# Moving a third block of an output weight from one wide load into small transfers issued by GpSimd

## The chip, the cores and the metric

One core of a Trainium2 chip. The metric is the device time of one execution in microseconds; the kernel before takes 680.46 us (median of 3 runs, 680.43 to 680.58).

## The reference

One decoding step, batch 8, width 512, all float32. The normalised input goes into a grouped-query attention over a cache of 4096 keys (32 heads, 8 key-value heads, 128 wide) and into a gated MLP; the result is `x + s * g`.

```python
xn = layernorm(x)                                   # [8, 1, 512]
# attention
q = (xn @ wq) -> 32 heads of 128
scores = q . k_cache * 128**-0.5                    # k_cache, v_cache: [8, 8, 4096, 128]
s = softmax(scores) . v_cache -> [8, 1, 4096] @ wo  # wq [512, 4096], wo [4096, 512]
# gated MLP
z = gelu(xn @ w_in)                                 # w_in [512, 1792]
z1, z2 = z[:896], layernorm(z[896:])
g = silu((z1 * (w_sp * z2 + b_sp)) @ w_out)         # w_out [896, 512]
out = x + s * g
```

## The kernel before, in words

All data passes once from HBM to SBUF: wq, w_mlp, the caches k and v, and wo. The bulk goes through a ring of three slots of 64 KB a partition (`slot()`, `bufs=3`). SP issues the loads in the order of the program: wq, x, `w_mlp` (w_in, part of w_out and some side data), four loads `w_ex0` to `w_ex3`, then for each of the 8 key-value heads two halves of k and two of v (8 MB each, 64 KB a partition), and at the end wo in pieces, the first one ahead of the last v. A load waits on SP until PE has finished with the slot that it takes. The first v load takes the slot of w_mlp, so it waits until the MLP is done with it.

For each head PE forms the scores (line 269), DVE and ACT the softmax, PE the values (line 310). The two projections of q (line 249) and the whole MLP (`mlp()`) run ahead of the first head. The last pieces of wo are multiplied as they arrive (`project_o`, `direct`), and the result is stored.

w_out has 896 rows, seven blocks of 128 (`NB`). The hidden vector u is held as four groups of 32 partitions (`G`, `R`) by 256 columns (`FQ`), so group g holds blocks 2g and 2g + 1. Two blocks (`MOVED`, blocks 1 and 3) are not in w_mlp. They are brought by the four w_ex loads into a few partitions of the tile `w_ex`, seven units (`UNITS`) of 512 columns side by side; the rest of `w_ex` is zeroed by GpSimd first (line 98). `LANES` gives for each load its place, its number of fours of partitions, and its units. The sources hold a fifth, unused row after each four, so that their leading dimension is the number of fours.

In the MLP the kept blocks are used through `hT`, two transposes of u (line 206, copied out at 207) with one product a block (line 224). For the moved blocks the columns of u are copied to matching columns of a zeroed tile `spread` (lines 210 and 213), which is transposed unit by unit (line 217), copied (`hE`, line 219) and multiplied with `w_ex` (line 228). All add up in `pw`.

GpSimd issues no DMA. It has memsets, a part of the identity and two powers (lines 149 and 199).

Of the kernel before, what the change touches and what calls it, by code (L numbers as in the profile page):

```python
# [1 line left out]

# [6 lines left out]
F32 = mybir.dt.float32  # L9
# [4 lines left out]
P = 128  # L14
B, D = 8, 512
HKV, REP, S, DH = 8, 4, 4096, 128
NK = D // P
G = 4
J = S // (G * P)
R = 32  # L20
FH = 896
FQ = 256
NB = FH // P
MOVED = 2
QUAD = 4
UNITS = 7
LANES = [(0, 5, 0, 6), (1, 5, 0, 5), (1, 3, 5, 2), (0, 3, 6, 1)]
EPS = 1e-5
GELU_C = 0.7978845608028654
HALF = B // 2  # L30
# [7 lines left out]
AHEAD = FOLDED + 2  # L38


def lane_runs():
    f = 0
    for e, k, u, n in LANES:
        m = k * QUAD
        at, end = f, f + n * m
        while at < end:
            g = at // P
            stop = min(end, (g + 1) * P)
            unit, lo = divmod(at - f, m)
            if lo or stop - at < m:  # L50
                whole, size = 1, min(m - lo, stop - at)
            else:
                whole, size = (stop - at) // m, m
            yield g, at - g * P, u + unit, whole, e * R + lo, size
            at += whole * size
        f = end


@with_exitstack
def tile_gqa_gmlp_decode(ctx: ExitStack, tc: tile.TileContext, x, kT, v, wq, wo, w_mlp, w_ex0, w_ex1, w_ex2, w_ex3, out, gate, stored):  # L60
    nc = tc.nc
    head = ctx.enter_context(tc.tile_pool(name="head", bufs=1))
    l = head.tile([P, HKV], F32, name="l")
# [4 lines left out]
    const = ctx.enter_context(tc.tile_pool(name="const", bufs=1))  # L68
# [5 lines left out]
    def slot():  # L74
        return ring.tile([P, SLOT], F32, name="slot")
# [5 lines left out]
    mlp_slot = slot()  # L81
    n_in, n_out = NK * 2 * FH, (NB - MOVED) * D
    n_mlp = n_in + n_out + P
    w_in_sb = mlp_slot[:, :n_in].rearrange("p (k n) -> p k n", k=NK)
    w_out_sb = mlp_slot[:, n_in:n_in + n_out].rearrange("p (j d) -> p j d", j=NB - MOVED)
    side_sb = mlp_slot[:, n_in + n_out:n_mlp]
    spare = [n_mlp]

    def from_slot(rows, n):
        lo = spare[0]  # L90
        spare[0] = lo + n
        return mlp_slot[:rows, lo:lo + n]
# [1 line left out]
    x_sb = from_slot(B, D)  # L94
    nc.sync.dma_start(x_sb, x)
    nc.sync.dma_start(mlp_slot[:, :n_mlp], w_mlp)
    w_ex = from_slot(2 * R, UNITS * D).rearrange("p (u d) -> p u d", u=UNITS)
    nc.gpsimd.memset(w_ex, 0.0)
    for (e, k, u, n), src in zip(LANES, (w_ex0, w_ex1, w_ex2, w_ex3)):
        nc.sync.dma_start(w_ex[e * R:e * R + k * QUAD, u:u + n], src[:, :QUAD])  # L100


    ident = const.tile([P, P], F32, name="ident")
    make_identity(nc, ident)
# [29 lines left out]
    def scratch(shape, name):  # L134
        t = ps.tile([P, 512], F32, name="scr")
        n = 1
        for s in shape[1:]:
            n *= s
        return t[:shape[0], :n]
# [18 lines left out]
    def mlp():  # L158
        zu = work.tile([P, 2, 2, FQ], F32, name="zu", tag="p")
        z, u_sb = zu[:, 0], zu[:, 1]  # L160
        rest = work.tile([P, 2 * D], F32, name="rest", tag="pT")
        hT, y_sb = rest[:, :2 * P], rest[:, D:]
        hT = hT.rearrange("p (a s) -> p a s", a=2)
        pz = scratch([P, 2 * FQ], "pz")
        nc.vector.memset(pz, 0.0)
        pz_v = pz.rearrange("p (a f) -> p a f", a=2)
        w_in_v = w_in_sb.rearrange("p k (a f) -> p k a f", a=2)
        for k in range(NK):
            for g in range(G):
                lo = g * FQ  # L170
                n = min(FQ, FH - lo)
                nc.tensor.matmul(pz_v[R * g:R * (g + 1), :, :n], xnT[:, k, :],
                                 w_in_v[:, k, :, lo:lo + n], start=(k == 0), stop=(k == NK - 1))
        zf, uf = z.rearrange("p a f -> p (a f)"), u_sb.rearrange("p a f -> p (a f)")
        nc.vector.tensor_copy(zf, pz)
        nc.vector.tensor_mul(uf, zf, zf)
        nc.vector.tensor_scalar(uf, uf, 0.044715, 1.0, op0=ALU.mult, op1=ALU.add)
        nc.vector.tensor_mul(uf, uf, zf)
        nc.scalar.activation(uf, uf, AF.Tanh, scale=GELU_C)
        nc.vector.tensor_scalar(uf, uf, 1.0, 0.5, op0=ALU.add, op1=ALU.mult)  # L180
        nc.vector.tensor_mul(zf, uf, zf)

        def mean(src, name, eps=0.0):
            part_sum = small.tile([P, 1], F32, name="part_sum")
            nc.vector.tensor_reduce(part_sum, src, op=ALU.add, axis=AX.X)  # L185
            pm = scratch([P, 1], "pm")
            nc.tensor.matmul(pm, same_all, part_sum, start=True, stop=True)  # L187
            t = small.tile([P, 1], F32, name=name)
            nc.vector.tensor_scalar(t, pm, 1.0 / FH, eps, op0=ALU.mult, op1=ALU.add)
            return t  # L190

        z1, z2 = z[:, 0, :], z[:, 1, :]
        mu = mean(z2, "mu")
        nc.vector.tensor_scalar(z2, z2, mu, None, op0=ALU.subtract)
        nc.vector.tensor_mul(u_sb[:, 0, :], z2, z2)
        nc.vector.memset(u_sb[(G - 1) * R:, 0, FH - (G - 1) * FQ:], 0.0)
        var = mean(u_sb[:, 0, :], "var", EPS)
        rs = small.tile([P, 1], F32, name="rs")
        nc.gpsimd.tensor_tensor(rs, var, neg_half, op=ALU.pow)
        nc.vector.tensor_scalar(z2, z2, rs, None, op0=ALU.mult)  # L200
        nc.vector.tensor_scalar(z2, z2, side_sb[:, W:W + 1], side_sb[:, W + 1:W + 2],
                                op0=ALU.mult, op1=ALU.add)
        nc.vector.tensor_mul(u_sb[:, 1, :], z2, z1)
        for a in range(2):
            th = scratch([P, P], "th")
            nc.tensor.transpose(th, u_sb[:, 1, a * P:(a + 1) * P], ident)  # L206
            nc.vector.tensor_copy(hT[:, a, :], th)
        wide = MOVED * R
        spread = from_slot(wide, UNITS * 2 * R).rearrange("p (u s) -> p u s", u=UNITS)
        nc.gpsimd.memset(spread, 0.0)  # L210
        for g, f, u, n, lo, m in lane_runs():
            rows = slice(R * g, R * (g + 1))
            nc.vector.tensor_copy(spread[rows, u:u + n, lo:lo + m],
                                  u_sb[rows, 1, P + f:P + f + n * m].rearrange("p (u s) -> p u s", u=n))
        te = scratch([2 * R, UNITS * wide], "te")
        for i in range(UNITS):
            nc.tensor.transpose(te[:, i * wide:(i + 1) * wide], spread[:, i, :], ident[:wide, :wide])  # L217
        hE = from_slot(2 * R, UNITS * wide)
        nc.vector.tensor_copy(hE, te)
        pw = scratch([P, D], "pw")  # L220
        kept = [j for j in range(NB) if j % 2 == 0 or j // 2 >= MOVED]
        for i, j in enumerate(kept):
            g, a = divmod(j, 2)
            nc.tensor.matmul(pw[R * g:R * (g + 1), :], hT[:, a, R * g:R * (g + 1)], w_out_sb[:, i, :],  # L224
                             start=(a == 0), stop=False)
        for i in range(UNITS):
            lo = wide * (i % 2)
            nc.tensor.matmul(pw[lo:lo + wide, :], hE[:, i * wide:(i + 1) * wide], w_ex[:, i, :],  # L228
                             start=False, stop=(i >= UNITS - 2))
        nc.vector.tensor_copy(y_sb, pw)  # L230
        py = scratch([P, W], "py")
        for g in range(G):
            for a in range(2):
                nc.tensor.matmul(py[R * g:R * (g + 1), :], pick[:, a, :],
                                 y_sb[:, (2 * g + a) * W:(2 * g + a + 1) * W], start=(a == 0), stop=(a == 1))
        nc.vector.tensor_copy(x_out, side_sb[:, :W])
        e = work.tile([P, W], F32, name="e", tag="o_all")
        nc.vector.tensor_scalar(e, py, -1.0, 87.0, op0=ALU.mult, op1=ALU.min)
        nc.scalar.activation(e, e, AF.Exp)
        nc.vector.tensor_scalar(e, e, 1.0, None, op0=ALU.add)  # L240
        nc.vector.reciprocal(e, e)
        nc.vector.tensor_mul(gate, py, e)
# [57 lines left out]
    turn = [0]  # L300
# [46 lines left out]
    project_q(0)  # L347
    project_q(1)
    mlp()
    for h in range(HKV):  # L350
        for half in range(2):
# [3 lines left out]
        for half in range(2):  # L355
# [11 lines left out]
            n = 2 if last else HALF  # L367
# [28 lines left out]
    for a in range(2):  # L396
        for g in range(G):
            c = (2 * g + a) * W
            nc.tensor.matmul(acc[R * g:R * g + OUT_ROWS, :], pick[:, a, :OUT_ROWS], part_f[:, c:c + W],
                             start=False, stop=False)  # L400
# [54 lines left out]
```

## Time and profile before

| | |
|---|---|
| median of 3 runs | 680.46 us (680.43 to 680.58) |
| profiled execution | 680.28 us |
| its span, first to last instruction | 678.8 us |
| granted TensorE clock, mean | 0.75 |
| busy PE / weight loads / DVE / ACT / GpSimd | 344.0 / 92.5 / 83.4 / 13.4 / 7.9 us |
| bytes read from HBM | 290.80 MB, 428 GB/s over the span |
| DMA packets | 6741, of which 6576 on the queue q1 |

The profile's DMA part has a row for each queue with packets, megabytes and the time of the packets as a share of sixteen engines' span. q1 holds the loads that SP issues, q8 and q14 the fetches of instructions, q10 the store at the end. A packet's record has a queue, a start, a duration and a size, and no engine number. In a view by stretches, the last two numbers of a row are the busy share of the sixteen DMA engines and the GB/s; packets are counted by their start, so that a share over a short stretch may pass 1.

### The profile page before, as it was taken

To read this page: it belongs to the slowest core of one execution; us is meant where nothing else is said; L and a number is where in the kernel's file an instruction comes from. 1 tells how busy PE (TensorE), PEld (TensorE's weight loads), DVE (VectorE), ACT (ScalarE), POOL (GpSimd) and SP (SyncE) were. 2 spreads that over 40 slices of the span, in tenths; PEclk is the share of its full clock that TensorE was granted. 3 is DMA by queue.
4 is the path that set the end of the run, shared out by engine and by line. 5 is a ranking of instruction groups with operands and counts; after the bars stand their busy time and mean duration, and the time that the engine had idled before them with its cause. 6 is when DMAs were issued, how large, how long until landed. Compare 5 with 4: busy or idle time off the path is not lost.

```text
span 678.8 us, 5218 instructions
## 1 busy us (share of the span) xinstructions
PE 344.0 (51%) x2415; PEld 92.5 (14%) x2415; DVE 83.4 (12%) x159; ACT 13.4 (2%) x27; POOL 7.9 (1%) x17
## 2 busy tenths in 40 slices
PE   0448744446655454555554344555544345555567
PEld 0112211111111011111111011111111011111111
DVE  1143021102110021101100021101101021100221
ACT  0010000000000000000000000000000000000000
POOL 3000000000000000000000000000000000000000
PEclk9987866787776568777666778877666787876679
DMA  9999999999999999999999999999999999999997
GB/s 386 453 441 430 430 433 430 433 430 433 434 433 430 433 433 430 433 441 440 434 433 430 436 436 434 440 434 433 430 433 430 433 433 434 430 436 433 419 427 315
DMA packets 6741, 291.16 MB, mean 429 GB/s; under 512 B 888, under 2 KB 888, under 8 KB 1688
## 3 DMA queue, kind: packets, MB, share of 16 engines
q1 hardware_dynamic: 6576, 290.80, 99.1%
q8 instruction: 19, 0.31, 0.2%
q10 hardware_dynamic: 144, 0.03, 0.0%
q14 instruction: 2, 0.02, 0.0%
HBM read 290.80 MB, written 0.03 MB: 428 GB/s over the span
## 4 chain that ended last, share of the span: by engine, by line
DMA 79%; PE 16%; issue 4%; DVE 0%; SPq 0%; POOLq 0%; POOL 0%
DMA slot<-in_kT 36%; DMA slot<-in_v 33%; PE sc L269 7%; PE o_ps L310 7%; DMA slot<-in_wo 7%; DMA slot<-in_x 3%; PE scr L224 1%; PE scr L228 1%; SPq L332 0%; PE scr L217 0%; DVE st L146 0%; POOLq L449 0%; POOL rstd L149 0%; PE scr L206 0%; PE acc L391 0%
## 5 line engine op out<-in xcount | busy, mean ns | idle before, releaser
L269 PE MATMUL sc<-slot,qz 128*32 128x512 f32 x1024 | 145.4, 731 | 131.2 <-DMA slot<-in_kT 131.2
L310 PE MATMUL o_ps<-slot,pT 128*16 128x512 f32 x1024 | 148.2, 743 | 110.0 <-DMA slot<-in_v 110.0
L269 PEld LDWEIGHTS sc<-slot,qz 128*32 128x32 f32 x1024 | 38.1, 131 | 232.0 <-issue 149.4
L310 PEld LDWEIGHTS o_ps<-slot,pT 128*16 128x16 f32 x1024 | 32.9, 114 | 211.0 <-issue 151.5
L274 DVE TENSOR_REDUCE nm<-sc 128x1 f32<-128x1024 f32 x8 | 9.8, 1225 | 273.7 <-PE sc L269 273.7
L313 DVE TENSOR_TENSOR o_all<-o_ps,diag 128x512 f32<-128x512 f32 x17 | 11.8, 692 | 244.8 <-PE o_ps L310 244.8
L276 ACT ACTIVATE p<-sc,nm 128x1024 f32<-128x1024 f32 x8 | 8.9, 1114 | 551.8 <-DVE nm L274 551.8
L320 PE MATMUL po_ps<-fold,o_sb 128*128 128x16 f32 x30 | 6.0, 274 | 26.8 <-DVE o_sb L315 26.8
L315 DVE TENSOR_REDUCE o_sb<-o_all 128x128 f32<-128x512 f32 x17 | 17.8, 1047 | 0.6
L153 PE MATMUL scr<-ident,slot 8*128 8x8 f32 x4 | 0.6, 254 | 25.0 <-DVE slot L150 25.0
L320 PEld LDWEIGHTS po_ps<-fold,o_sb 128*128 128x128 f32 x30 | 4.5, 189 | 40.6 <-DVE o_sb L315 40.6
L296 DVE STREAM_TRANSPOSE pT<-p 128x1024 f32<-128x1024 f32 x8 | 10.0, 1246 | 0.3
L249 PE MATMUL scr<-slot,xnT 128*32 128x512 f32 x64 | 8.9, 708 | 0.3 <-issue 0.3
L344 PE MATMUL sc<-slot,oT 128*8 128x512 f32 (+1 forms) x60 | 8.4, 565 | 1.1 <-DMA slot<-in_wo 1.0
L279 PE MATMUL scr<-ident,nm 128*1 128x128 f32 x8 | 2.2, 270 | 10.8 <-DVE nm L274 10.8
L292 PE MATMUL scr<-wl,same 128*128 128x1 f32 x16 | 3.6, 297 | 6.5 <-DVE wl L290 6.5
L294 DVE TENSOR_SCALAR p<-p,w,wl 128x1024 f32<-128x1024 f32 x8 | 6.5, 813 | 0.3
L224 PE MATMUL scr<-slot,rest 128*32 128x512 f32 x10 | 5.4, 1044 | 0.0
L187 PE MATMUL scr<-part_sum,same 128*128 128x1 f32 x4 | 1.1, 348 | 8.4 <-DVE part_sum L185 8.4
L285 PE MATMUL scr<-ident,full 1*128 1x1 f32 x8 | 1.8, 220 | 5.0 <-DVE full L283 5.0
L292 PEld LDWEIGHTS scr<-wl,same 128*128 128x128 f32 x16 | 3.2, 249 | 7.0 <-PE scr L285 7.0
L153 PEld LDWEIGHTS scr<-ident,slot 8*128 8x128 f32 x4 | 0.5, 208 | 25.0 <-DVE slot L150 25.0
(94 smaller groups left out, 69.0 us busy)
## 6 DMA issues: line engine op xcount, KB each, us to landing
slot<-in_v SPq DMA_DIRECT2D x2, 4096.0 KB, 28.7
slot<-in_w_mlp SPq DMA_DIRECT2D x1, 4928.0 KB, 32.7
slot<-in_wo SPq DMA_DIRECT2D x1, 2048.0 KB
slot<-in_wo SPq DMA_DIRECT2D x1, 1536.0 KB
slot<-in_wo SPq DMA_DIRECT2D x1, 1280.0 KB, 37.9
slot<-in_wo SPq DMA_DIRECT2D x1, 1024.0 KB
slot<-in_wo SPq DMA_DIRECT2D x4, 256.0 KB, 18.7
slot<-in_wo SPq DMA_DIRECT2D x1, 768.0 KB
```

Source lines behind the costliest of these rows:

```text
L224: nc.tensor.matmul(pw[R * g:R * (g + 1), :], hT[:, a, R * g:R * (g + 1)], w_out_sb[:, i, :], start=(a == 0), stop=False)
L249: nc.tensor.matmul(pq[R * g:R * (g + 1), :], xnT[:, k, :], wq_sb[:, k, lo:lo + REP * DH], start=(k == 0), stop=(k == NK - 1))
L269: nc.tensor.matmul(sc[R * g:R * (g + 1), c, :], qz[:, h, b * R:(b + 1) * R], k_sb[:, i, c, g, :], start=(b == 0), stop=(b == B - 1))
L274: nc.vector.tensor_reduce(m, sc, op=ALU.max, axis=AX.XY, negate=True)
L276: nc.scalar.activation(p, sc.rearrange("p c s -> p (c s)"), AF.Exp, bias=m, accum_out=l[:, h:h + 1])
L292: nc.tensor.matmul(tot, same_all, wl, start=True, stop=True)
L296: nc.vector.transpose(pT.rearrange("p j b g r -> p j g b r"), p.rearrange("p (j g b r) -> p j g b r", j=J, g=G, b=B))
L310: nc.tensor.matmul(of[R * c:R * c + G * REP, :], pT[:, j, b0 + i], v_sb[:, i, j], start=(j < rows), stop=(j >= J - rows))
L313: nc.vector.tensor_mul(o_all, o, diag[:, :, None].to_broadcast([P, G, DH]))
L315: nc.vector.tensor_reduce(o_sb, o_all.rearrange("p g d -> p d g"), op=ALU.add, axis=AX.X)
L320: nc.tensor.matmul(po[:, b0 * REP:(b0 + n) * REP], o_sb, f.rearrange("p i r -> p (i r)"), start=True, stop=True)
L344: nc.tensor.matmul(part[R * q:R * q + B, i * n:(i + 1) * n], oT[:, h, r, :], wo_sb[:, m, i * n:(i + 1) * n], start=(m < REP), stop=(cuts = ...
```

## The change

`MOVED` goes from 2 to 3: block 5 leaves w_mlp as well. Its rows are brought by GpSimd-issued transfers: `w_mid` into partitions 60 to 67, and `w_one0` to `w_one3` into three partitions each. Between these stand four transfers `skip` of a few bytes from w_mlp into a tile `turn` that nothing reads. The nine are kept in their written order (`tc.issue_after`). By the words of the change, the five are transfers of one and two shares into the partitions of DMA engines 7, 8 and 15: w_mid is two shares, of engines 7 and 8, and the w_ones are one share each, of engine 15, 7, 8 and 15 in this order.

`w_ex` now spans 128 partitions, its zeroing too. The four loads on SP bring the same bytes to the same partitions as before, but which row of w_out lies where has changed: a list `RUNS`, written out, gives for each run of columns its group, first column, first unit, units, first partition and count. `spread` has 32 rows instead of 64 and 128 columns a unit instead of 64; it is filled by 11 copies instead of 6. The unit's product has 32 stationary columns instead of 64 and adds to one group of `pw`; which group follows from the unit's number. One transpose of u remains of two, and four kept products of five.

In the order of instructions, the first skip is GpSimd's first work after the constants; the zeroing of `w_ex` and a memset of the identity follow, then the other eight transfers (the ninth waits for the first one's completion), and then the rest of the identity, the memsets and the first power. On DVE, the sums built from the identity (same, fold, diag) now stand behind the statistics of x and ahead of the instruction that normalises x. SP's order is unchanged.

```diff
-MOVED = 2
+MOVED = 3
 QUAD = 4
 UNITS = 7
-LANES = [(0, 5, 0, 6), (1, 5, 0, 5), (1, 3, 5, 2), (0, 3, 6, 1)]
+LANES = [(0, 20, 0, 6), (32, 20, 0, 5), (32, 12, 5, 2), (0, 12, 6, 1)]
+ONES = [(93, 0, 7), (29, 0, 5), (96, 0, 5), (124, 0, 7)]
+RUNS = [(0, 0, 0, 6, 0, 20), (0, 120, 0, 1, 60, 8), (1, 0, 0, 5, 29, 23), (1, 115, 6, 1, 0, 12),
+        (1, 127, 0, 1, 124, 1), (2, 0, 1, 6, 60, 8), (2, 48, 5, 2, 32, 12), (2, 72, 0, 5, 93, 6),
+        (2, 102, 5, 2, 93, 3), (2, 108, 0, 1, 125, 2), (2, 110, 1, 6, 124, 3)]
...
-    w_ex = from_slot(2 * R, UNITS * D).rearrange("p (u d) -> p u d", u=UNITS)
+    w_ex = from_slot(P, UNITS * D).rearrange("p (u d) -> p u d", u=UNITS)
     nc.gpsimd.memset(w_ex, 0.0)
-    for (e, k, u, n), src in zip(LANES, (w_ex0, w_ex1, w_ex2, w_ex3)):
-        nc.sync.dma_start(w_ex[e * R:e * R + k * QUAD, u:u + n], src[:, :QUAD])
+    for (p, m, u, n), src in zip(LANES, (w_ex0, w_ex1, w_ex2, w_ex3)):
+        nc.sync.dma_start(w_ex[p:p + m, u:u + n], src[:, :QUAD])
+    turn = const.tile([4 * QUAD, 4, QUAD], F32, name="turn")
+    queued = []
+
+    def queue(dst, src):
+        with tc.issue_after(queued[-1]) if queued else nullcontext():
+            queued.append(nc.gpsimd.dma_start(dst, src).ins)
+
+    def skip(i, k):
+        queue(turn[:2 * k, i], w_mlp[:k, :4 * QUAD].rearrange("p (a q) -> p a q", a=2)[:, :, :QUAD])
+
+    def one(i, src):
+        p, u, n = ONES[i]
+        queue(w_ex[p:p + 3, u:u + n].rearrange("p u d -> p (u d)").rearrange("p (c n) -> p c n", c=2),
+              src[:, :3, :n * D // 2])
+
+    skip(0, 7)
+    queue(w_ex[60:68], w_mid[:, :QUAD])
+    skip(1, 6)
+    one(0, w_one0)
+    skip(2, 7)
+    one(1, w_one1)
+    one(2, w_one2)
+    skip(3, 6)
+    one(3, w_one3)
...
-        for a in range(2):
-            th = scratch([P, P], "th")
-            nc.tensor.transpose(th, u_sb[:, 1, a * P:(a + 1) * P], ident)
-            nc.vector.tensor_copy(hT[:, a, :], th)
-        wide = MOVED * R
-        spread = from_slot(wide, UNITS * 2 * R).rearrange("p (u s) -> p u s", u=UNITS)
+        th = scratch([P, P], "th")
+        nc.tensor.transpose(th, u_sb[:, 1, :P], ident)
+        nc.vector.tensor_copy(hT, th)
+        spread = from_slot(R, UNITS * P).rearrange("p (u s) -> p u s", u=UNITS)
         nc.gpsimd.memset(spread, 0.0)
-        for g, f, u, n, lo, m in lane_runs():
-            rows = slice(R * g, R * (g + 1))
-            nc.vector.tensor_copy(spread[rows, u:u + n, lo:lo + m],
-                                  u_sb[rows, 1, P + f:P + f + n * m].rearrange("p (u s) -> p u s", u=n))
-        te = scratch([2 * R, UNITS * wide], "te")
+        for g, f, u, n, p, m in RUNS:
+            nc.vector.tensor_copy(spread[:, u:u + n, p:p + m],
+                                  u_sb[g * R:(g + 1) * R, 1, P + f:P + f + n * m].rearrange("p (u s) -> p u s", u=n))
+        te = scratch([P, UNITS * R], "te")
         for i in range(UNITS):
-            nc.tensor.transpose(te[:, i * wide:(i + 1) * wide], spread[:, i, :], ident[:wide, :wide])
-        hE = from_slot(2 * R, UNITS * wide)
+            nc.tensor.transpose(te[:, i * R:(i + 1) * R], spread[:, i, :], ident[:R, :R])
+        hE = from_slot(P, UNITS * R)
         nc.vector.tensor_copy(hE, te)
         pw = scratch([P, D], "pw")
-        kept = [j for j in range(NB) if j % 2 == 0 or j // 2 >= MOVED]
-        for i, j in enumerate(kept):
-            g, a = divmod(j, 2)
-            nc.tensor.matmul(pw[R * g:R * (g + 1), :], hT[:, a, R * g:R * (g + 1)], w_out_sb[:, i, :],
-                             start=(a == 0), stop=False)
+        for g in range(G):
+            nc.tensor.matmul(pw[R * g:R * (g + 1), :], hT[:, R * g:R * (g + 1)], w_out_sb[:, g, :],
+                             start=True, stop=False)
         for i in range(UNITS):
-            lo = wide * (i % 2)
-            nc.tensor.matmul(pw[lo:lo + wide, :], hE[:, i * wide:(i + 1) * wide], w_ex[:, i, :],
-                             start=False, stop=(i >= UNITS - 2))
+            g = (i + 2) % G
+            nc.tensor.matmul(pw[R * g:R * (g + 1), :], hE[:, i * R:(i + 1) * R], w_ex[:, i, :],
+                             start=False, stop=(i >= UNITS - G))
```

The host side lays the sources out to match: `w_mid` as two shares of four rows and an unused fifth, each `w_one` as 2 x 3 half rows with an unused fourth and some padding.

More of the change, by code (lines that the diff above doesn't have):

```diff
@@ L1 @@
-from contextlib import ExitStack
+from contextlib import ExitStack, nullcontext
 import concourse.bass as bass
@@ L38, with tile_gqa_gmlp_decode @@
 AHEAD = FOLDED + 2
[L41 to L56, printed above, removed]
 @with_exitstack
-def tile_gqa_gmlp_decode(ctx: ExitStack, tc: tile.TileContext, x, kT, v, wq, wo, w_mlp, w_ex0, w_ex1, w_ex2, w_ex3, out, gate, stored):
+def tile_gqa_gmlp_decode(ctx: ExitStack, tc: tile.TileContext, x, kT, v, wq, wo, w_mlp, w_ex0, w_ex1, w_ex2, w_ex3, w_mid, w_one0, w_one1, w_one2, w_one3, out, gate, stored):
     nc = tc.nc
@@ L161, in mlp @@
         rest = work.tile([P, 2 * D], F32, name="rest", tag="pT")
-        hT, y_sb = rest[:, :2 * P], rest[:, D:]
-        hT = hT.rearrange("p (a s) -> p a s", a=2)
+        hT, y_sb = rest[:, :P], rest[:, D:]
         pz = scratch([P, 2 * FQ], "pz")
@@ L423, with padded @@
     moved = list(range(1, 2 * MOVED, 2))
-    rows = w_out[moved].reshape(MOVED * P, D)
-    w_ex, f = {}, 0
-    for i, (e, m, u, n) in enumerate(LANES):
-        t = np.zeros((m, QUAD + 1, n, D), np.float32)
-        t[:, :QUAD] = rows[f:f + n * m * QUAD].reshape(n, m, QUAD, D).transpose(1, 2, 0, 3)
-        w_ex[f"w_ex{i}"] = t.reshape(m, QUAD + 1, n * D)
-        f += n * m * QUAD
+    rows = w_out[moved]
+    extra = np.zeros((P, UNITS, D), np.float32)
+    for g, f, u, n, p, m in RUNS:
+        extra[p:p + m, u:u + n] = rows[g, f:f + n * m].reshape(n, m, D).transpose(1, 0, 2)
+    def padded(t, k):
+        t = t.reshape(k, t.shape[0] // k, -1)
+        return np.pad(t, ((0, 0), (0, 1), (0, 0)))
+    w_ex = {f"w_ex{i}": padded(extra[p:p + m, u:u + n], m // QUAD) for i, (p, m, u, n) in enumerate(LANES)}
+    w_ex["w_mid"] = padded(extra[60:68], 2)
+    for i, (p, u, n) in enumerate(ONES):
+        t = extra[p:p + 3, u:u + n].reshape(2, 3, -1)
+        w_ex[f"w_one{i}"] = np.pad(t, ((0, 0), (0, 1), (0, QUAD)))
     arrays = {
```

## The prediction

> **What bounds the kernel now.** I read the page first: span, DMA queues, then the chain that ended last.
>
> ```profile
> span 678.8 us, 5218 instructions
> DMA  9999999999999999999999999999999999999997
> q1 hardware_dynamic: 6576, 290.80, 99.1%
> q8 instruction: 19, 0.31, 0.2%
> DMA 79%; PE 16%; issue 4%; DVE 0%; SPq 0%; POOLq 0%; POOL 0%
> ```
>
> The sixteen DMA engines are busy in every slice, and the one load queue (q1, issued by SP) takes 99.1% of 16 x 678.8 us, that is 10,763 us for 290.80 MB: 27.0 GB/s an engine, or 2.43 us for a row of 64 KB (65,536 bytes). PE's 16% of the chain is the recycling of slots in the steady part, where loads queue ahead. So the last loaded byte sets the end, and the second thing to read is that end: the timeline, the chain in order of time, and the busy time by stretches of the last 6 us.
>
> ```profile
> 675.61 0.42 PE L391 MATMUL acc<-slot,oT_last 128*16 128x64 f32 x16
> 676.25 0.42 PE L391 MATMUL acc<-slot,oT_last 128*16 128x64 f32 x16 [0.22 <-DMA slot<-in_wo]
> 665.08 11.13 DMA slot<-in_wo
> 676.25 0.46 PE acc L391 x16
> 670.60:671.40 0.80, 0.80 (x8) 0.10 (x8) 0.00 (x0) 0.00 (x0) 0.00 (x0) 1.00 1.02 417
> 672.00:674.00 2.00, 1.33 (x14) 0.23 (x14) 0.00 (x0) 0.00 (x0) 0.00 (x0) 1.00 0.84 330
> 675.20:675.60 0.40, 0.40 (x31) 0.23 (x18) 0.00 (x0) 0.00 (x0) 0.00 (x0) 1.00 0.42 164
> 675.70:676.00 0.30, 0.30 (x16) 0.15 (x16) 0.00 (x0) 0.00 (x0) 0.00 (x0) 1.00 0.10 34
> ```
>
> In the last four rows the two last numbers are the DMA share and GB/s. The share falls from 1.02 to 0.84 between 671.4 and 672 us (13 of 16 would be 0.81), is 0.42 (about seven engines) at 675.2 to 675.6, and 0.10 after 675.7. So three engines run dry near 671.7 us, some 4.1 us before the last ones at about 675.8 us; all hold the same share of each 128-row load, so what differs is the rest: the w_ex rows and the fetches of q8. PE waits only 0.22 us for the last piece of wo, but its earlier pieces are waited for too, so the tail moves with the loads.
>
> **The change, part by part.** One more block of w_out (128 x 512 floats, 262,144 bytes) leaves the load of w_mlp: 2048 bytes a partition, 16,384 bytes an engine, 0.61 us at 27.0 GB/s, on each of the sixteen. It comes back, by the change's own words, on three engines only. Engines 7 and 8 each get half of w_mid (4 rows of 14,336 bytes) and one w_one (6 rows of 5,120): 88,064 bytes, 3.26 us in 10 rows. Engine 15 gets two w_one of 6 rows of 7,168 bytes: 86,016 bytes, 3.18 us in 12 rows. If these are the three that run dry early, each is 3.2 - 0.6 = 2.6 us later, still 1.5 us ahead of the old end, and the late ones are 0.61 us earlier. That is the whole possible gain: nothing takes a byte more off the late engines.
>
> What the transfers cost besides their bytes is the open term. The trace has no DMA issued by GpSimd. The nearest rows are those where a packet of another queue comes between two rows of q1. Four answers of the DMA view, each over a window of 0.02 us that holds the start of one packet; the share times 16 x 0.02 us is that packet's time.
>
> ```profile
> q14 instruction: 1, 0.01, 96.6%
> q1 hardware_dynamic: 1, 0.07, 921.6%
> q8 instruction: 1, 0.02, 287.8%
> q1 hardware_dynamic: 1, 0.07, 914.1%
> ```
>
> The first two are from 58.67 and 58.97 us: 8 KB of q14 took 0.31 us, its bytes at full rate, and the 64 KB row of q1 after it 2.95 us in place of 2.43. The last two, from 103.67 and 104.57 us: 16 KB of q8 took 0.92 us (0.61 at full rate), and the q1 row after it 2.93 us. So the return to q1 cost 0.50 to 0.52 us both times, and the fetch of q8 another 0.31. A stream that is broken into loses half a microsecond on that engine; rows of one queue lose nothing.
>
> A GpSimd row of 5 to 14 KB between rows of q1 is the same situation, unless a backlog of its own queue lets the engine prepare both sides ahead. The bounds are 0 (as within q1) and 0.81 us a row; a gain is excluded, for the bytes are the same. I take 0.50 us, the return that both kinds of foreign packet show, and one return for each row, since each fetch went between two single 64 KB rows. Engine 15 then ends 3.18 - 0.61 + 12 x 0.50 - 4.1 = 4.5 us after the old end; engines 7 and 8: 3.26 - 0.61 + 10 x 0.50 - 4.1 = 3.6 us. The later decides: +4.5 us. With half of the returns it is 3.18 - 0.61 + 3.0 - 4.1 = +1.5; with 0.81 each, 3.18 - 0.61 + 9.7 - 4.1 = +8.2.
>
> [...] The trace's fetches slip in after one row, so I keep the row count.
>
> The four skip transfers move a few bytes each, but they too are foreign packets, on engines that the texts of the change leave unnamed; two on one late engine at 0.50 us each would be +1.0 - 0.61 = +0.4 us.
>
> **The chain of the MLP.** It runs beside the loads, and matters only if the first load of v is issued too late.
>
> ```profile
> 0.88 3.08 POOL L98 MEMSET slot<- 64x3584 f32 x1
> 1.56 0.35 SPq L96 DMA_DIRECT2D slot<-in_w_mlp  x1
> 3.98 3.25 SPq L100 DMA_DIRECT2D slot<-in_w_ex  x4
> 4.32 0.37 DVE L111 TENSOR_REDUCE same<-ident 128x32 f32<-128x128 f32 x1 [2.30 <-POOL ident masks.py:199]
> 5.04 0.15 DVE L121 TENSOR_REDUCE fold_last<-fold 128x8 f32<-128x16 f32 x1
> 6.87 0.47 POOL L210 MEMSET slot<- 64x448 f32 x1
> 22.66 0.68 DVE L146 BATCH_NORM_STATS2 st<-slot 8x6 f32<-8x512 f32 x1 [17.47 <-DMA slot<-in_x]
> 24.39 0.53 DVE L150 TENSOR_SCALAR slot<-slot,mv,rstd 8x512 f32<-8x512 f32 x1 [0.67 <-POOL rstd L149]
> 24.98 0.59 PE L153 MATMUL scr<-ident,slot 8*128 8x8 f32 x4 [24.98 <-DVE slot L150]
> 63.98 8.39 SPq L332 DMA_DIRECT2D slot<-in_v  x2
> slot<-in_w_mlp SPq DMA_DIRECT2D x1, 4928.0 KB, 32.7
> L213 DVE COPY slot<-zu 32x12 f32<-32x12 f32 (+4 forms) x6 | 0.8, 172 | 0.1
> L207 DVE COPY rest<-scr 128x128 f32<-128x128 f32 x2 | 0.5, 292 | 0.1
> L224 PE MATMUL scr<-slot,rest 128*32 128x512 f32 x10 | 5.4, 1044 | 0.0
> ```
>
> POOL: nine DMA issues stand among its first instructions, with the affine select of the identity, the memsets and the first power behind them. An issue of w_ex on SP took 3.25 / 4 = 0.81 us; nine of these are 7.3 us, and at double that 14.6. POOL was done by 7.3 us, so it ends by 15 to 22, before the identity is used at 24.98: hidden. The ninth waits for the first one's completion, which was issued ahead of the 3.08 us memset; nothing for SP hangs on it but its four w_ex issues, which wait for the memset and are late by one issue, with 20 us of wq queued in front.
>
> DVE: the builds of same, fold and diag now stand behind the statistics of x, so they no longer run while x is awaited: five instructions from 4.32 to 5.19, 0.9 us, against 0.67 in which DVE waits for the power there anyway. And x itself lies behind wq on the engine that takes shares. I allow 0.5 us for the first and 2.5 to 5.5 us for the second (the shares that fit between wq's eight rows, without and with returns). In the MLP, eleven spread copies for six add 5 x 0.17 = 0.9 us, one transposed copy less takes 0.29 off, and two of ten passes of L224 less take 2 x 1.04 = 2.1 off. So the v load goes out at 63.98 + 0.5 + (2.5 to 5.5) - 1.5 = 65.5 to 68.5. w_mlp lands at 1.56 + 32.7 = 34.3, and two K loads of 8 rows each keep an engine busy for 16 x 2.43 = 38.9 us more: 72 to 73 us, and no more than 0.6 earlier. Cover of 3 us or more is left, so zero; where it were gone, each microsecond would first eat the spare time of engines that end early.
>
> **The sum.** On the profiled execution (680.28 us, of which 678.8 span and 1.48 around it): 680.28 + 4.5 = 684.8. The median of the runs is 0.18 above that execution, so 684.9 us, 0.65% slower. About 0.2% (1.4 us) is what a measurement of this kernel can tell from no change.
>
> **Rivals.**
> *The return costs nothing for a GpSimd queue, or once a transfer.* For it: the 0.50 us was seen with instruction fetches alone, single packets that arrive unannounced, where the new transfers come with a backlog; against it: it was there at both fetch queues. Without a price the late engines end 0.61 us earlier, 680.46 - 0.6 = 679.9; with one return a transfer the skips decide, +0.4, 680.9. This one is not slower by what can be measured. It decides when the cost a row falls below (4.1 - 2.6 + 1.4) / 12 = 0.24 us. Chance 0.43.
>
> *Every engine pays for every transfer.* A completion has to be told. If each of the nine transfers puts a packet on all sixteen engines, the late ones pay 9 x 0.50 - 0.61 = +3.9 us even if the rows were free: 684.4; with the rows' returns on engine 15 and seven such packets more, +8.0, 688.4. Nothing in this trace shows a GpSimd completion; chance 0.08. [...]
>
> *The shares land elsewhere.* The placement hangs on nine transfers taking turns on the engines in a fixed order from a known start; the trace before can't show that. If a share of 3.2 us falls on a late engine, the end is 3.2 - 0.6 = +2.6 us later, 683.1, without any return. Chance 0.06. A start that is off would show as late engines with unchanged early ones.
>
> **How the numbers follow.** Forecast (the return price on rows of the three engines, 682.0 to 688.6 by its bounds): 0.41; no or one return, 679.9 to 680.9: 0.43 in all, but of these the free one 0.33 and one return a transfer 0.10, so the forecast is the likeliest single case; every engine pays: 0.08; elsewhere: 0.06; a gain over 1.4 us, which the 0.61 us bound rules out unless fetches move: 0.02. Slower 0.41 + 0.08 + 0.06 = 0.55, same 0.43, faster 0.02. The range goes from 679.8, just under the free case, to 688.0; the forecast's own is 682.0 to 688.6.
>
> **What would show it.** Right: the q1 rows after GpSimd packets near 2.9 us in the first 40 us; in the last stretches the DMA share falling in the other order, thirteen engines dry by about 675.3 and three at work until about 680. Wrong: a share that stays near 1 until 674 and falls within 2 us (no price); a share near 1 until 679 (all engines pay); the v load issued after 72 us with the share dropping there would break the cover of the MLP.

## The result, and the profile after

| | median | lowest to highest | runs |
|---|---|---|---|
| before | 680.52 us | 680.43 to 680.66 | 4 |
| changed | 689.78 us | 689.62 to 690.01 | 4 |

The changed kernel is 9.26 us slower: ratio 1.0136, 95% interval 1.0119 to 1.0154. Its profiled execution took 689.62 us with a span of 688.0 us, 9.2 us more than before. The forecast was 684.9 us in 679.8 to 688.0: slower was right, but the size was not, and the cause is one that the prediction had put at zero.

The page of the changed kernel, the lines that answer to those of before; the third is the throughput in 40 slices of 17.2 us.

```profile
span 688.0 us, 5236 instructions
DMA  9999599999999999999999999999999999999997
GB/s 403 414 437 426 231 428 473 434 424 427 424 438 431 428 434 451 434 424 427 439 442 424 431 446 439 427 428 427 443 427 427 447 442 439 428 427 428 427 416 289
q1 hardware_dynamic: 6576, 290.54, 97.8%
q0 software_dynamic: 656, 0.27, 0.1%
DMA 73%; PE 18%; issue 4%; another core or an unknown queue 3%; DVE 1%; POOL 0%; SPq 0%; POOLq 0%
L231 PE MATMUL scr<-slot 128*32 128x512 f32 x14 | 3.6, 1058 | 11.8 <-DMA slot<-in_w_one 11.8
```

The whole loss is in one place: the fifth slice, 69 to 86 us, moves 231 GB/s where its neighbours move over 420. The last row names the wait: the product with `w_ex` stood 11.8 us for a w_one. (The chain has the same wait, 11.74 us from 64.18 on, as "another core or an unknown queue".) The timeline around it, and the same stretch by windows (last two numbers: DMA share, GB/s):

```profile
25.13 0.68 DVE L155 BATCH_NORM_STATS2 st<-slot 8x6 f32<-8x512 f32 x1 [23.11 <-DMA slot<-in_x]
62.35 0.39 DVE L224 COPY slot<-scr 128x224 f32<-128x224 f32 x1 [3.01 <-PE scr L222]
76.01 3.64 PE L231 MATMUL scr<-slot 128*32 128x512 f32 x14 [11.84 <-DMA slot<-in_w_one]
79.76 0.33 SPq L335 DMA_DIRECT2D slot<-in_v  x1
60.00:71.00 11.00, 4.18 (x14) 0.90 (x12) 0.39 (x1) 0.00 (x0) 0.00 (x0) 0.50 0.93 397
72.00:74.00 2.00, 0.00 (x0) 0.00 (x0) 0.00 (x0) 0.00 (x0) 0.00 (x0) 0.50 0.55 237
74.00:75.50 1.50, 0.00 (x0) 0.00 (x0) 0.00 (x0) 0.00 (x0) 0.00 (x0) 0.50 0.05 19
75.50:80.00 4.50, 3.64 (x14) 0.68 (x14) 0.28 (x1) 0.00 (x0) 0.00 (x0) 0.50 0.00 0
```

The product could have run at 64.2 us (76.01 - 11.84). It ran at 76.0, the MLP let go of its slot at 79.8, and only then did SP issue the first v load, 15.8 us later than before. The two k loads ahead of it had run out by then. By the packet records seven engines end their last row of k between 71.7 and 72.0 us, near the 72 to 73 that the prediction had counted, and the other nine between 73.5 and 76.2; the view counts a row where it starts, so its share is zero from 75.5 to 80. The first rows of the v load start between 80.7 and 81.6. The seven that were first stood about 9 us without data, about the size of the loss.

Why were the transfers so late? GpSimd had issued them all by 11.4 us (the last issue of line 92 begins at 10.75). The DMA view over short windows shows it: first 26 to 28 us, during w_mlp, then 44 to 46.42 us, one row of a k load on each engine.

```profile
q1 hardware_dynamic: 29, 1.08, 125.2%
q0 software_dynamic: 29, 0.01, 1.6%
q1 hardware_dynamic: 16, 1.05, 99.9%
q0 software_dynamic: 13, 0.01, 0.8%
```

In the first window as many packets of the GpSimd queue (q0) start as of SP's (q1): here the engines take the two queues in turn, one packet each, and a packet of q1 is a whole row of a partition, up to 64 KB and 2.42 us (in the records 4096 of the 6576 are of 65,536 bytes, 32 loads of 128 rows). So a GpSimd packet of a few bytes waits for a row. (In the second window three rows of q1 follow the row before directly: in the records, these three engines had taken more turns beside the short rows of w_ex and have no GpSimd packet left.)

And there are many: 656 on the page, 41 times sixteen, where the five w transfers have 4 x 2 + 4 x 6 = 32 rows of data in all. The sizes in the packet records tell what the others are. The four skips have 64, of 8 or 32 bytes, one on each engine. The remaining 560 are of 4 bytes. The records don't say what for, but a simple count gives this number: a completion of each of the nine transfers on all sixteen engines (144), and a filler on every engine without a share for each row that an engine with one takes (4 x 14 = 56 for w_mid, 4 x 6 x 15 = 360 for the w_ones). So by this count every transfer costs every engine as many turns as its share has rows, and a turn more: 2 for each skip, 5 for w_mid, 7 for each w_one; 8 + 5 + 28 = 41. Two runs below with fewer transfers agree: 512 packets on the page of one, 16 x 32 (41 - 2 - 7), and 400 on that of the other, 16 x 25. At up to 2.42 us a turn the last share cannot land much before the queue of SP is empty: in the records the last packet of q0 starts at 75.29 us, and the last row of k ends at 76.2.

### The profile page after: what moved, and what is told of

It reads as the page before. It is cut to its first block, busy times and chain, and to the rows that moved or that the text cites. A ratio compares the mean times of both kernels' runs of the same rounds, so it can differ in the third digit from the quotient of the medians.

```text
span 688.0 us, 5236 instructions
## 1 busy us (share of the span) xinstructions
PE 341.1 (50%) x2412; PEld 91.8 (13%) x2412; DVE 83.7 (12%) x163; ACT 13.4 (2%) x27; POOL 14.5 (2%) x26
## 3 DMA queue, kind: packets, MB, share of 16 engines
q1 hardware_dynamic: 6576, 290.54, 97.8%
## 4 chain that ended last, share of the span: by engine, by line
DMA 73%; PE 18%; issue 4%; another core or an unknown queue 3%; DVE 1%; POOL 0%; SPq 0%; POOLq 0%
DMA slot<-in_kT 35%; DMA slot<-in_v 28%; PE sc L272 11%; DMA slot<-in_wo 7%; PE o_ps L313 6%; DMA slot<-in_x 3%; PE scr L227 1%; PE scr L231 1%; DVE slot L218 0%; PE scr L222 0%; POOL pick L134 0%; POOL slot L216 0%; SPq L335 0%; DVE rest L233 0%
## 5 line engine op out<-in xcount | busy, mean ns | idle before, releaser
L272 PE MATMUL sc<-slot,qz 128*32 128x512 f32 x1024 | 147.1, 739 | 127.0 <-DMA slot<-in_kT 127.0
L313 PE MATMUL o_ps<-slot,pT 128*16 128x512 f32 x1024 | 144.5, 728 | 110.5 <-DMA slot<-in_v 108.1
L316 DVE TENSOR_TENSOR o_all<-o_ps,diag 128x512 f32<-128x512 f32 x17 | 11.8, 692 | 241.7 <-PE o_ps L313 241.7
L231 PE MATMUL scr<-slot 128*32 128x512 f32 x14 | 3.6, 1058 | 11.8 <-DMA slot<-in_w_one 11.8
```

The source lines that it names most:

```text
L231: nc.tensor.matmul(pw[R * g:R * (g + 1), :], hE[:, i * R:(i + 1) * R], w_ex[:, i, :], start=False, stop=(i >= UNITS - G))
L272: nc.tensor.matmul(sc[R * g:R * (g + 1), c, :], qz[:, h, b * R:(b + 1) * R], k_sb[:, i, c, g, :], start=(b == 0), stop=(b == B - 1))
L313: nc.tensor.matmul(of[R * c:R * c + G * REP, :], pT[:, j, b0 + i], v_sb[:, i, j], start=(j < rows), stop=(j >= J - rows))
L316: nc.vector.tensor_mul(o_all, o, diag[:, :, None].to_broadcast([P, G, DH]))
```

## The experiments

**Shorter rows on SP's queue, with the control.** If a turn lasts as long as a row of SP's queue, shorter rows give the same transfers faster turns.

```diff
-    nc.sync.dma_start(wq_sb, wq)
+    for c in range(8):
+        n = SLOT // 8
+        nc.sync.dma_start(wq_sb[:, c * n:(c + 1) * n], wq[:, c * n:(c + 1) * n])
```

> The changed kernel, with the load of wq issued as eight loads of an eighth of the columns (rows of 8 KB in place of 64 KB on the queue of SP). Theory A, one packet of the GpSimd queue after each row of the SP queue: an engine needs 41 turns for its 41 GpSimd packets, a row of wq now takes 0.31 us, so all shares land by about 23 us, the product with w_ex does not wait, the first v load is issued near 68 us and the queue never runs dry: 679.9 to 680.6 us. Theory B, the GpSimd queue has a pace of its own of about 2.4 us a packet: w_ex lands near 75 us as before, 689 us. Theory C, the price of 0.5 us for each return to the SP queue, as the prediction had it: 41 returns on each engine, 690 us or more.

Measured: 680.12 us (680.0 to 680.82, 11 runs) against 680.49 of before on the same chip (27 runs), ratio 0.9996, interval 0.9987 to 1.0004. The 9.3 us are gone, with all 41 packets an engine still there. Theories B and C fall: the GpSimd queue shows no pace of 2.4 us a packet of its own (474 of its packets start in 10 us, 29.6 an engine), and 41 returns cost no 20 us. The DMA view of this kernel from 8 to 18 us, and its v load:

```profile
q1 hardware_dynamic: 548, 3.99, 94.8%
q0 software_dynamic: 474, 0.20, 7.1%
68.50 8.39 SPq L337 DMA_DIRECT2D slot<-in_v  x2
```

474 GpSimd packets in 10 us, where the changed kernel has 29 in 2 us; its last one starts at 23.3 us in the records, in place of 75.3 in the changed kernel. The same edit on the kernel before:

> The kernel before with the same eight loads of wq, as the control: under every theory 680.5 to 680.8 us; seven more completions of some 10 ns on each engine.

680.44 us (680.25 to 681.09, 11 runs), ratio 1.0001, interval 0.9992 to 1.001. So the short rows give nothing by themselves, and the third block, with the wait gone, is worth 0.32 us by the medians (680.12 and 680.44); the intervals don't tell that from nothing. Where it goes can be seen at the end of the span. First the control, then the changed kernel with eight loads:

```profile
672.00:673.00 1.00, 1.00 (x14) 0.20 (x7) 0.00 (x0) 0.00 (x0) 0.00 (x0) 1.00 0.85 340
673.00:674.00 1.00, 1.00 (x8) 0.09 (x1) 0.00 (x0) 0.00 (x0) 0.00 (x0) 1.00 0.84 328
675.40:675.80 0.40, 0.40 (x32) 0.40 (x32) 0.07 (x1) 0.00 (x0) 0.00 (x0) 1.00 0.47 179
```

```profile
672.00:673.00 1.00, 1.00 (x10) 0.19 (x6) 0.00 (x0) 0.00 (x0) 0.00 (x0) 1.00 1.02 401
673.00:674.00 1.00, 0.95 (x12) 0.12 (x8) 0.00 (x0) 0.00 (x0) 0.00 (x0) 1.00 1.05 404
675.40:675.80 0.40, 0.38 (x20) 0.24 (x16) 0.00 (x0) 0.00 (x0) 0.00 (x0) 1.00 0.06 21
```

The three engines' worth of share that was missing from 672 us on is there until about 674, and the last engines end some 0.4 us earlier. The records have no engine number, but this is what the shares on the three idle engines would look like.

**Two loads of wq.** A smaller dose.

> The changed kernel with wq in two loads (rows of 32 KB). Theory A: six more turns before the SP queue runs out of rows near 72 us, 40 in place of 34, so the last share lands near 71 us in place of 75, the v load goes out near 75.5 in place of 79.8: 685 us (684 to 686.5). Theory B: 689 us. Theory C: 690 us or more.

Measured: 689.27 us (688.92 to 689.61, 4 runs). The expected 685 was missed, and theory B's 689 was met, though the kernel with eight loads had refuted B. The turns did come faster at first, but the product still began late (the view names no releaser for it here):

```profile
75.77 3.64 PE L233 MATMUL scr<-slot 128*32 128x512 f32 x14 [9.38 <-issue]
79.52 0.33 SPq L337 DMA_DIRECT2D slot<-in_v  x1
```

The mistake was the end of the count. I took 34 turns as all that the changed kernel has before 72 us and credited six more. But the engine of the last w_one (15, by the change) has its own 3.2 us of shares, so its SP rows last until about 75. In the records the last w_one's six rows start at 59.0 to 72.4 us here, 2.7 us apart, one a turn, and the last completion follows at 75.3. In the changed kernel the same six start at 73.65 to 74.99, 0.27 us apart, when that engine's SP queue is empty and no turn is left to wait for. Two ways to the same 75.3 us. That left a third theory: the last completion comes when SP's queue has run dry, however many packets there are. The next two runs tell that apart.

**Fewer packets, rows as they were.**

```diff
-    skip(3, 6)
-    one(3, w_one3)
```

> The changed kernel without its last skip and last w_one (its rows stay zero in w_ex, so that part of the MLP is left out): 32 GpSimd packets an engine in place of 41. Theory A, one turn a row of the SP queue: the third w_one is the last, its rows ended at 67.8 us in the changed kernel and its completion follows near 70.4; the product starts near 70.6 in place of 76.0, the v load goes out near 74.3 in place of 79.8: 684.3 us (683.3 to 685). Theory D, the last GpSimd completion comes only when the SP queue has run dry, whatever the count: 689 us.

Measured: 684.79 us (683.93 to 684.94, 4 runs), against 684.3 (683.3 to 685) of theory A and 689 of D.

```profile
70.65 3.44 PE L229 MATMUL scr<-slot 128*32 128x512 f32 x14 [8.17 <-DMA slot<-in_w_one]
74.23 8.39 SPq L333 DMA_DIRECT2D slot<-in_v  x2
```

The product starts at 70.65 (expected 70.6), the v load goes out at 74.23 (expected 74.3).

```diff
-    one(2, w_one2)
-    skip(3, 6)
-    one(3, w_one3)
```

> The same without the last two w_ones and the last skip: 25 packets an engine. Theory A: the second w_one is the last, complete near 53 us, ahead of the product, which starts near 64; the v load goes out near 68 us and the queue does not run dry: 680.0 to 680.5 us. Theory D: 688 to 689 us.

Measured: 680.08 us (680.0 to 680.35, 10 runs) against 680.47 of before on the same chip, interval 0.9985 to 1.0004. The last GpSimd packet starts at 54.5 us in the records, the v load goes out at 64.97 us (earlier than the 68 expected), and there is no wait for a w_one. With 64 KB rows, 25 packets an engine are hidden, 32 cost 4.3 us, 41 cost 9.3: the time follows the number of packets, and theory D falls.

**Transfers that nobody waits for.**

```diff
+DQ = D // 4
...
+    unread = const.tile([P, UNITS * DQ], F32, name="unread")
...
+    queue(unread[60:68], w_mid[:, :QUAD])
```

> The kernel before with the same nine GpSimd transfers in the same order, with rows of a quarter of the length, into a tile that nothing reads and that holds no slot: packets and turns without the wait. Theory A: the GpSimd packets are served until about 100 us, nobody waits for them, and they cost their own 10 to 15 ns each, 0.4 to 0.6 us on every engine: 680.9 to 681.1 us. Theory B: 680.5 to 681.1 us as well. Theory C: 41 x 0.5 us on each engine, 690 to 701 us.

Measured: 680.82 us (680.74 to 680.97, 11 runs), 0.33 above before and just under the 680.9 to 681.1 of theory A; the interval, 0.9997 to 1.0015, does not tell it from no change.

```profile
q0 software_dynamic: 368, 0.07, 0.1%
```

The shorter rows went as 23 packets an engine (368 / 16) and were through by 49 us, not 100, so the kernel is no equal of the changed one in its count. Theories A and B had overlapping ranges, and it does not tell them apart. It still decides on theory C: 23 returns at 0.5 us would be 11.5 us.

**Without the skips.** Eight loads of wq, and the four skip transfers left out.

> The kernel with eight loads of wq (which measured 680.1) without the four skips, nothing else: tests that the skips set where the shares land. If each transfer takes the engines next in turn from the first one on, the two shares of w_mid (57 KB each) and the four w_ones (30 or 43 KB) now fall on the first six engines, five of which are late ones: the latest ends 2.1 us later than it does with the skips, 682.2 us (681.6 to 682.8). If the skips don't matter, 680.0 us.

Measured: 684.88 us (684.8 to 685.11, 5 runs): 4.8 us above the kernel with skips, where 2.1 was expected. So the skips matter, and the end is drawn out as it would be with shares on engines that were late already: the DMA share is still 0.66 from 676 to 677 us and 0.12 from 680 to 681. That the skips do it by placing the shares fits, but is not seen directly, and the price was under-sized. From 8 to 18 us, as above for the kernel with skips:

```profile
q1 hardware_dynamic: 419, 3.06, 93.9%
q0 software_dynamic: 390, 0.22, 9.6%
```

A packet of SP's queue now takes 0.359 us (93.9% of 160 us / 419) in place of 0.277 (94.8% / 548). The rows of wq themselves go slower while the shares move: in the records an 8 KB row takes 0.31 us throughout this stretch in the kernel with skips, and 0.50 in the mean from 10 to 14 us here. The first two slices of the two pages (17 us each) show what that costs: 321 and 419 GB/s here, 368 and 454 with skips, some 1.4 MB less, which at 428 GB/s is an estimated 3 us of the 4.8. Why the rows go slower no run here shows.

**Four loads of wq.**

> The changed kernel with four loads of wq (rows of 16 KB). Theory A: about 24 turns of 0.6 us before wq is in, the other 17 at rows of w_mlp, of 1.4 us: the shares land by 45 us, ahead of the product: 680.1 us, as with eight loads. Theory D: 689 us.

Measured: 680.18 us (680.07 to 680.3, 11 runs) against 680.47, interval 0.9986 to 1.0004; the v load goes out at 67.48. Four loads do as well as eight, and neither is a gain that these runs can tell from none.

## Why the prediction was wrong

- **Bytes and placement: right, as far as the runs show.** Three engines had 4 us to spare, and with the wait gone (eight loads of wq) the shares fitted in and the late ones end earlier. The 0.61 us bound holds: 0.32 to 0.37 by the medians. The packets' own time can account for the rest: 41 packets of 9 ns in the records are 0.37 us an engine. The medians do not tell this closer.
- **The return price: wrong.** The forecast stood on 0.50 us for each return to SP's queue, taken from instruction fetches. Three windows of the changed kernel, the first of 0.01 us at 12.30, the others of 0.005 and 0.01 at 12.84 and 13.03, hold one packet each:

```profile
q0 software_dynamic: 1, 0.01, 334.4%
q1 hardware_dynamic: 1, 0.07, 3022.5%
q1 hardware_dynamic: 1, 0.07, 1511.2%
```

  A row of 14,336 bytes took 0.535 us, its bytes at full rate, and the 64 KB rows of q1 that start as two such end took 2.418 us both (3022.5% of 16 x 0.005, 1511.2% of 16 x 0.01): no return price. Of the 320 rows of 64 KB that start between 12 and 74 us, 318 took 2.42 us; the two others, of 2.99 and 2.90, come behind the two instruction fetches of that stretch. The first rival had the price right. Why a fetch costs it and a GpSimd packet does not, no run shows.
- **The step that failed: "Cover of 3 us or more is left, so zero".** It priced the first v load from x and the MLP's own instructions, 65.5 to 68.5 us. Without the wait it would have gone out at 67.9 (79.76 - 11.84), so that part was right; x came 2.5 us later (25.13 against 22.66), the low end of what was allowed. The step never asked when the shares land. They landed at 75.3 us, and the term put at zero was worth the whole 9.3. The prediction did say that a row goes between two rows of SP, and used it for a price alone: twelve turns of 2.4 us are 29 us on engine 15 before a single filler is counted. The text even took the shares to fit between wq's eight rows. The sign that it named for this, a v load issued after 72 us with the share dropping there, is what came. That the kernel got slower, as forecast, is luck: the price that the forecast stood on is nil, and with the landing early enough the same transfers gave 680.12 us.
- **The number of packets: wrong.** 10 and 12 rows were counted for the three engines. By the count above all sixteen have 41. The second rival had every engine touched by every transfer, but priced it by returns; the harm is the turns. The pages agree with sixteen equal counts (656 = 16 x 41 in the changed kernel, 368 = 16 x 23 in the run whose rows nobody reads), and a turn is a single row of SP's queue (29 packets to 29 from 26 to 28 us).
- **Shares elsewhere:** nothing points to it. The run without skips, where by its expectation six engines get a share, came out 4.4 us above before (684.88 against 680.47), not 2.6; it is no exact test of that rival, which has one share on a late engine.

## What to carry to other kernels

In this kernel a small transfer on a second queue did not cost its bytes, it cost turns: packets an engine times the time of one row of the big queue, and that is when it landed: the last packet started at 75.3 us beside rows of up to 2.42 us, and at 23.3 us beside rows of wq of 0.31 us, 41 packets an engine both times. Before moving data to such a queue, count the packets on every engine, multiply, and follow who waits for the landing. Where rows of the big queue are as long as here, cutting one load into shorter rows can bring the landing forward: four loads of wq did (680.18 us), at no cost that these runs could tell, and two did not (689.27 us).

## What the runs showed of the hardware that was not expected

In these traces an engine served the two queues in turn (29 packets to 29 in 2 us) whatever the sizes, so 4 bytes waited for 64 KB (2.42 us), and by the count a GpSimd transfer with a share on one engine put as many packets on the other fifteen (656 in all, 16 x 41). A GpSimd packet left the following row at 2.42 us, while an instruction fetch lengthened it to 2.90 to 2.99. Without the skips, the packets of SP's queue went from 0.277 to 0.359 us while the shares moved; the cause is open.
